# Diagonal score blocks: the lower left quarter mirrored through memory, with a new order of pairs and of the chunk steps

## The chip, the cores and the metric

One core of a Trainium2 chip runs the whole kernel. The metric is the device time of one execution in microseconds: 1388.75 us before the change, the median of three runs (1388.1 to 1389.97).

## The reference

Attention with a squared Relu, multiplied by u, then a mixture of experts in which only 80 tokens of each expert count:

```python
scores = scale * np.matmul(z, z.transpose(0, 2, 1))   # z: 8 x 2496 x 64, scale 1/2496
attn = np.maximum(scores, 0.0) ** 2
x = u * np.matmul(attn, v)                            # u, v: 8 x 2496 x 256
...
logits = x @ w_gate                                   # x as 19968 x 256, 8 experts
expert_idx = np.argmax(logits, axis=1)
gate_w = probs[np.arange(N), expert_idx]              # softmax of the logits
for e in range(E):                                    # the 80 tokens with the largest gate_w
    h = np.maximum(x[tok_idx] @ w1[e], 0.0)
    out[tok_idx] = gate_w[tok_idx, None] * (h @ w2[e])
```

The score matrix of a batch is z times its own transpose, so it is symmetric: the block of rows i and columns j is the transpose of the block of rows j and columns i.

## The kernel before

Attention fills the first 1300 us. It runs over 8 batches, in each over 5 chunks of 512 query columns (`qc`; the last one has 448), and in each chunk over 10 **steps**. A step handles one **pair** of key tiles of 128 (tiles 2p and 2p+1, step number `r`). `pairs_of` (L246) gives the order of the pairs of a chunk: 0 to 9, in the fourth chunk 8, 9, 0 to 7.

All the work of PE, ScalarE, VectorE and of SP's queue is in the order in which it is written (`manual_schedule`, L765); each engine runs its own list in order and waits by semaphores. In step i the main loop (L777) writes down first the `scores` of the pair of step i + 2 (`LOOK`), then `attend` of the pair of step i, then what is due for the chunk before (`finished`), then loads and preparations.

`scores` (L315) makes the pair's squared-Relu tile `a` (128 keys x 2 x 512 queries) and splits it in a high part `ah` and a rest `al`, so that f32 accuracy comes from reduced f32 matmuls:

- For a key tile of the chunk's own diagonal block or to the right of it: two matmuls (`zc`, `zd`: high and rest of z) into a PSUM tile `s`, Relu (ScalarE, L330), Square over both tiles (L331), `ah` as a copy (ScalarE, or VectorE where `on_v`), `al` as a subtraction (VectorE, L54).
- For a block to the left of the diagonal nothing is computed: its transpose was computed in an earlier chunk. Then `mirror` had VectorE transpose it by 32x32 (L265), `mirror_out` wrote it to memory as `y` two steps later (L275), and `mirror_back` read it again in four pieces as `blk` (L292), at most 12 steps ahead of its use, when one of four buffers is free and the write is two steps old. `mirrored` (L299) then takes only a ScalarE copy and a VectorE subtraction.

`attend` (L344) multiplies with the value tiles `vt` (also high and rest): three matmuls for each of two halves of the model dimension, 12 a step, into `acc`; the last key tile takes four instead of six. `ah` and `al` have three buffers, `a` two, `s` three.

After a chunk, `chunk_x` (VectorE, L377) multiplies `acc` with u into `xf` at step 0 of the next chunk. `finished` (L721) then spreads over the steps of the next chunk: `chunk_hi`, `chunk_rest`, `chunk_mid`, `chunk_lo` (three bf16 parts of x), `chunk_store` (two DMA transposes of `xf`, L427), `chunk_store2` (their result to memory, L436), `chunk_logits` (24 small matmuls) and `chunk_sum`. After a batch come `gate_top` (with an exponential on ScalarE, L483), `gate_near` and `gate_sum`, `count` (matmuls and a copy into `tot`), `up_to` (ten small VectorE additions) and `blocks`.

For the next batch, z is loaded (`load_z`, one buffer, L100) at step 1 and prepared at step 5 of each chunk; the value tiles are loaded (`load_v`, two buffers, L132) from the fourth chunk on and prepared (`prep_v`, a ScalarE copy and a VectorE subtraction) at steps 2, 4, 6, 8 and 9 of the fifth. `prep_u` loads u at step 2, into one buffer that `chunk_x` reads.

The last 80 us, the experts, are not touched.

## Time and profile before

| | |
|---|---|
| median of 3 runs | 1388.75 us |
| profiled execution, its own time | 1388.46 us |
| its span, first to last instruction | 1386.6 us |
| mean granted TensorE clock over the span | 0.992 |
| PE busy | 99% |
| VectorE (DVE) busy | 76% |
| ScalarE (ACT) busy | 73% |
| DMA moved | 311.89 MB |

PE is TensorE's matmuls, PEld its weight loads, DVE VectorE, ACT ScalarE, SPq the queue of SP, which issues all the large DMAs. Matmuls are pipelined and their ends are modelled, so the distance from one start to the next is what one costs. A wait is named by the instruction that waited and the one that released it.

### The profile page before, as it was taken

What the parts mean: (1) busy time and instruction counts of PE and PEld (TensorE: products, weight loads), DVE (VectorE), ACT (ScalarE), POOL (GpSimd) and SP (SyncE); (2) the same over time, 40 slices, a digit from 0 to 9 for tenths busy, and PEclk for the clock granted to TensorE, in tenths of its full rate; (3) what the DMA queues carried; (4) which work ended last, traced back from release to release, by engine and by line L of the source; (5) the groups of instructions that cost most, each with busy time, mean ns of one, the idle gap of its engine ahead of it and who ended that gap; (6) DMA issues with size and microseconds to landing.
All of it is one profiled execution on the core that took longest, in us unless ns stands there. A gap on an engine that the chain in (4) does not pass through costs nothing. (4 is left out here: it accounts for less than half of the span.)

```text
span 1386.6 us, 19562 instructions
## 1 busy us (share of the span) xinstructions
PE 1367.1 (99%) x7087; PEld 1139.5 (82%) x7087; DVE 1060.6 (76%) x1517; ACT 1008.8 (73%) x1282; POOL 36.5 (3%) x57
## 2 busy tenths in 40 slices
PE   9999999999999999999999999999999999999887
PEld 6888888888888888888888888888888888888666
DVE  8876788668877788767886688777787678867785
ACT  8866687758777587666887577775877668876375
POOL 0000000000000000000000000000000000000062
PEclk9999999999999999999999999999999999999989
DMA  6899877995888958997688958889588986789774
GB/s 223 252 249 271 225 204 239 235 267 143 256 237 231 273 151 245 239 261 197 188 252 232 270 143 259 238 225 274 145 246 239 255 210 179 220 229 252 176 225 141
DMA packets 260070, 311.89 MB, mean 225 GB/s; under 512 B 96152, under 2 KB 188192, under 8 KB 249728
## 3 DMA queue, kind: packets, MB, share of 16 engines
q1 hardware_dynamic: 258752, 309.02, 81.4%
q0 software_dynamic: 1216, 1.56, 0.4%
q8 instruction: 57, 0.93, 0.3%
q14 instruction: 45, 0.37, 0.1%
HBM read 153.48 MB, written 126.37 MB: 202 GB/s over the span
## 5 line engine op out<-in xcount | busy, mean ns | idle before, releaser
L359 PE MATMUL acc<-ah,vt 128*128 128x512 f32 (+1 forms) x1520 | 584.5, 385 | 0.3 <-DVE vt L146 0.3
L360 PE MATMUL acc<-al,vt 128*128 128x512 f32 (+1 forms) x1520 | 584.5, 385 | 0.3 <-DVE al L54 0.2
L358 PE MATMUL acc<-ah,vt 128*128 128x512 f32 (+1 forms) x1520 | 584.2, 384 | 0.0
L54 DVE TENSOR_TENSOR al<-a,ah 128x1024 fp32r<-128x1024 f32 (+1 forms) x240 | 291.5, 1214 | 135.4 <-ACT ah L105 125.6
L330 ACT ACTIVATE a<-s 128x512 f32<-128x512 f32 (+1 forms) x480 | 258.4, 590 | 153.9 <-PE s L327 143.8
L359 PEld LDWEIGHTS acc<-ah,vt 128*128 128x128 f32 x1520 | 285.4, 188 | 53.9 <-DVE vt L146 1.2
L358 PEld LDWEIGHTS acc<-ah,vt 128*128 128x128 f32 x1520 | 285.3, 188 | 52.9
L360 PEld LDWEIGHTS acc<-al,vt 128*128 128x128 f32 x1520 | 285.4, 188 | 52.9 <-DVE al L54 1.2
L331 ACT ACTIVATE a<-a 128x1024 f32<-128x1024 f32 (+1 forms) x240 | 253.0, 1054 | 7.6
L310 ACT CAST ah<-blk 128x1024 fp32r<-128x1024 f32 x160 | 167.0, 1049 | 105.6 <-PE acc L359 88.5
L54 DVE TENSOR_TENSOR al<-blk,ah 128x1024 fp32r<-128x1024 f32 x160 | 193.8, 1216 | 56.1 <-ACT ah L310 53.2
L265 DVE STREAM_TRANSPOSE x<-a 128x512 f32<-128x512 f32 x320 | 207.6, 687 | 0.0
L327 PE MATMUL s<-zd,zc 128*128 128x512 f32 (+1 forms) x480 | 186.5, 388 | 0.0
L105 ACT CAST ah<-a 128x1024 fp32r<-128x1024 f32 x153 | 160.9, 1052 | 4.8
L107 DVE CAST ah<-a 128x1024 fp32r<-128x1024 f32 (+1 forms) x87 | 59.2, 681 | 95.6 <-ACT a L331 95.6
L326 PE MATMUL s<-zc,zc 128*128 128x512 f32 x320 | 128.1, 400 | 0.0
L327 PEld LDWEIGHTS s<-zd,zc 128*128 128x128 f32 x480 | 90.3, 188 | 16.3 <-issue 0.5
L326 PEld LDWEIGHTS s<-zc,zc 128*128 128x128 f32 x320 | 60.1, 188 | 11.1
L326 PE MATMUL s<-zc 128*128 128x512 f32 (+1 forms) x160 | 63.5, 397 | 0.0
L388 ACT CAST xb<-xf 128x1024 bf16<-128x1024 f32 (+1 forms) x39 | 40.0, 1026 | 23.4 <-DVE xf L377 23.1
L396 ACT CAST xb<-xr 128x1024 bf16<-128x1024 f32 (+1 forms) x39 | 39.9, 1024 | 15.5 <-DVE xr L54 15.5
L377 DVE SCALAR_TENSOR_TENSOR xf<-acc,ut 128x512 f32<-128x512 f32 (+2 forms) x82 | 50.1, 653 | 0.0
(171 smaller groups left out, 835.9 us busy)
## 6 DMA issues: line engine op xcount, KB each, us to landing
y<-x SPq DMA_DIRECT2D x80, 1024.0 KB
blk<-y SPq DMA_DIRECT2D x320, 256.0 KB
out<-idle SPq DMA_DIRECT2D x40, 512.0 KB
vraw<-v SPq DMA_DIRECT2D x32, 512.0 KB
ut<-uT SPq DMA_DIRECT2D x32, 512.0 KB
xs<-xq SPq DMA_DIRECT2D x32, 512.0 KB
wraw<-w SPq DMA_DIRECT2D x28, 512.0 KB
zd<-zc SPq DMA_DIRECT2D x78, 128.0 KB
```

The costliest lines, as they stand in the source:

```text
L54: V.tensor_tensor(out=o, in0=a, in1=b, op=op)
L105: eng.copy(out=o, in_=i)
L107: eng.tensor_copy(out=o, in_=i)
L265: V.transpose(out=x[:, :, :, t].rearrange("p n k s -> p k n s"), in_=a)
L310: nc.scalar.copy(out=natural(ah), in_=src)
L326: nc.tensor.matmul(s[:, :nq], zk, zc[:, :nq], start=True, stop=False)
L327: nc.tensor.matmul(s[:, :nq], zk, zd[:, :nq], start=False, stop=True)
L330: nc.scalar.activation(out=a[:, h, :nq], in_=s[:, :nq], func=AF.Relu)
L331: nc.scalar.activation(out=a[:, :, :nq], in_=a[:, :, :nq], func=AF.Square)
L358: nc.tensor.matmul(o, vt[:, t, 0, cs], ah, start=k == first, stop=False)
L359: nc.tensor.matmul(o, vt[:, t, 1, cs], ah, start=False, stop=False)
L360: nc.tensor.matmul(o, vt[:, t, 0, cs], al, start=False, stop=k == last)
```

## The change

In all diagonal blocks but three (the first chunk of the first batch and the last two chunks of the last batch) the second pair's scores are computed for the right half of the block's columns only. The left half is the transpose of the right half of the first pair, which is now computed first in its chunk. VectorE transposes that half by 32x32 (`quarter_out`), SP writes it to memory at step 0 (`quarter_write`) and reads it back at step 3 (`quarter_back`), and the second pair, now the last of its chunk, takes it from there with a copy and a subtraction (`natural`).

The order of pairs in such a chunk becomes: first diagonal pair, all others, second diagonal pair. The steps of the chunk's later work move: DMA transposes from step 1 to 4, their store from 3 to 6, logits from 6 to 7 (6 after the fifth chunk), gate from 7 and 8 to 8 and 9, count from 2 to 5, prefix sums and blocks from 4 to 9. z of the next batch is loaded one chunk later (in the fifth chunk two of them); the value tiles are prepared at steps 1, 3, 6 and 8 of the fifth chunk and, the last one, at step 3 of the next batch's first chunk. `tot` is bf16, and `ex` takes the place of `lg`.

```diff
--- before.py
+++ after.py
@@ -225,7 +225,7 @@
     oh = const.tile([P, 2, NBLK, E], BF16, name="oh")
     gall = const.tile([P, NCOL - NT + 32], F32, name="gall")
     nsum = const.tile([P, B + 1], F32, name="nsum")
-    tot = const.tile([P, E, NBLK], F32, name="tot")
+    tot = const.tile([P, E, NBLK], BF16, name="tot")
     incl = const.tile([P, E, NBLK], F32, name="incl")
     rank = const.tile([P, NST, E], F32, name="rank")
     ex_last = const.tile([P, NT, E], F32, name="ex_last")
@@ -243,8 +243,19 @@
     NP = NT // 2
 
 
-    pairs_of = [list(range(NP)) for qc in range(NQ)]
-    pairs_of[NQ - 2] = [NP - 2, NP - 1, *range(NP - 2)]
+    def whole_block(b, qc):
+        return (b, qc) in ((0, 0), (B - 1, NQ - 2), (B - 1, NQ - 1))
+
+    def order(b, qc):
+        rest = [p for p in range(NP) if p // 2 != qc]
+        if whole_block(b, qc):
+            return [NP - 2, NP - 1, *range(NP - 2)] if qc == NQ - 2 else list(range(NP))
+        if qc == NQ - 2:
+            rest = rest[-2:] + rest[:-2]
+        return [2 * qc, *rest, 2 * qc + 1]
+
+    pairs_of = {(b, qc): order(b, qc) for b in range(B) for qc in range(NQ)}
+    HQ = CH // 2
     LOOK, AHEAD = 2, 12
     a_t = {}
 
@@ -254,7 +265,7 @@
     n32 = P // SQ
     now, to_write = [0], []
 
-    to_read = [(b, i, j, (b * NQ + i) * NP + pairs_of[i].index(2 * j) - LOOK)
+    to_read = [(b, i, j, (b * NQ + i) * NP + pairs_of[b, i].index(2 * j) - LOOK)
                for b in range(B) for i in range(NQ) for j in range(i)]
 
     def mirror(b, i, j, t, a):
@@ -293,6 +304,33 @@
                                   in_=y[:, :, h].rearrange("g p f -> p g f"))
             blk[b, i, j] = m
 
+    quarter = {}
+
+    def quarter_out(b, qc, a):
+
+        x = zpool.tile([P, n32, 2, 2, SQ], F32, tag="md", name=f"xd_{b}_{qc}", bufs=1)
+        for t in range(2):
+            V.transpose(out=x[:, :, :, t].rearrange("p n k s -> p k n s"), in_=a[:, t, HQ:])
+        quarter[b, qc] = now[0], x
+
+    def quarter_write():
+
+        for (b, qc), (at, x) in list(quarter.items()):
+            if at is not None and at + 2 <= now[0]:
+                y = dram.tile([n32, SQ, n32, 4 * SQ], F32, tag="yd", name=f"yd_{b}_{qc}", bufs=2)
+                nc.sync.dma_start(out=y.rearrange("g p h f -> (g p) (h f)"),
+                                  in_=x.rearrange("p h k t s -> p (h k t s)"))
+                quarter[b, qc] = None, y
+
+    def quarter_back(b, qc):
+
+        _, y = quarter.pop((b, qc))
+        m = zpool.tile([P, n32, 2, 2 * SQ], F32, tag="md", name=f"md_{b}_{qc}", bufs=1)
+        for h in range(n32):
+            nc.sync.dma_start(out=m[h * SQ:(h + 1) * SQ].rearrange("p g k f -> p g (k f)"),
+                              in_=y[:, :, h].rearrange("g p f -> p g f"))
+        quarter[b, qc] = None, m
+
     def pair_tile(tag, b, qc, k, dt=F32R, bufs=3):
         return ew.tile([P, 2, CH], dt, tag=tag, name=f"{tag}_{b}_{qc}_{k}", bufs=bufs)
 
@@ -318,22 +356,35 @@
             return mirrored(b, qc, k)
         nq = min(CH, seq - qc * CH)
         zc, zd = zc_t[b, qc], zd_t[b, qc]
+        diag = k // QT == qc and not whole_block(b, qc)
+        lower = diag and k % QT > 0
+        c0, c1 = (HQ, nq) if lower else (0, CH if diag else nq)
         a = pair_tile("a", b, qc, k, F32, 2)
         ss = []
         for h in range(2):
             zk = zc_t[b, k // QT][:, (k % QT + h) * P:(k % QT + h + 1) * P]
             s = ps_s.tile([P, CH], F32, tag="s", name=f"s_{b}_{qc}_{k + h}")
-            nc.tensor.matmul(s[:, :nq], zk, zc[:, :nq], start=True, stop=False)
-            nc.tensor.matmul(s[:, :nq], zk, zd[:, :nq], start=False, stop=True)
+            nc.tensor.matmul(s[:, c0:c1], zk, zc[:, c0:c1], start=True, stop=False)
+            nc.tensor.matmul(s[:, c0:c1], zk, zd[:, c0:c1], start=False, stop=True)
             ss.append(s)
         for h, s in enumerate(ss):
-            nc.scalar.activation(out=a[:, h, :nq], in_=s[:, :nq], func=AF.Relu)
-        nc.scalar.activation(out=a[:, :, :nq], in_=a[:, :, :nq], func=AF.Square)
+            nc.scalar.activation(out=a[:, h, c0:c1], in_=s[:, c0:c1], func=AF.Relu)
+        nc.scalar.activation(out=a[:, :, c0:c1], in_=a[:, :, c0:c1], func=AF.Square)
         ah = pair_tile("ah", b, qc, k)
+        al = pair_tile("al", b, qc, k)
+        if lower:
+            m = quarter.pop((b, qc))[1].rearrange("p n k (t s) -> p k t n s", t=2)
+
+            def natural(o):
+                return o[:, :, :HQ].rearrange("p k (t n s) -> p k t n s", t=2, s=SQ)
+
+            nc.scalar.copy(out=natural(ah), in_=m)
+            tt(natural(al), m, natural(ah), ALU.subtract)
         on_v = k // QT == qc or (qc, k) in ON_V and b > 0
-        cp(V if on_v else nc.scalar, ah[:, :, :nq], a[:, :, :nq])
-        al = pair_tile("al", b, qc, k)
-        tt(al[:, :, :nq], a[:, :, :nq], ah[:, :, :nq], ALU.subtract)
+        cp(V if on_v else nc.scalar, ah[:, :, c0:nq], a[:, :, c0:nq])
+        tt(al[:, :, c0:nq], a[:, :, c0:nq], ah[:, :, c0:nq], ALU.subtract)
+        if diag and not lower:
+            quarter_out(b, qc, a)
         if k // QT > qc:
             for h in range(2):
                 mirror(b, k // QT, qc, k % QT + h, a[:, h])
@@ -343,7 +394,7 @@
 
     def attend(b, qc, k, cols=range(DC)):
         nq = min(CH, seq - qc * CH)
-        first, last = 2 * pairs_of[qc][0], 2 * pairs_of[qc][-1] + 1
+        first, last = 2 * pairs_of[b, qc][0], 2 * pairs_of[b, qc][-1] + 1
         if k == first:
             acc_t[b, qc] = [ps_a.tile([P, CH], F32, tag="acc", name=f"acc_{b}_{qc}_{c}")
                             for c in range(DC)]
@@ -479,7 +530,7 @@
         last = b == B - 1
         d = d_last if q1 == NQ and last else small("d")
         tt(d, lg, bc(mx), ALU.subtract)
-        ex = ex_last[:, q0 * QT:q1 * QT] if last else small("ex")
+        ex = ex_last[:, q0 * QT:q1 * QT] if last else lg
         nc.scalar.activation(out=ex, in_=d, func=AF.Exp)
 
         fw = small("fw")
@@ -685,6 +736,9 @@
     RAW = {(qz, 4): (2, 1), None: (2, 2)}
     WARM = 3, 6
     WARM0 = 8
+    keys_in = {qc: [(qc - 1, 1, 6)] for qc in range(1, NQ)}
+    keys_in[0] = []
+    keys_in[NQ - 1] = [(NQ - 2, 1, 4), (NQ - 1, 4, 7)]
     steps = [(b, qc, r) for b in range(B) for qc in range(NQ) for r in range(NP)]
     ET = mybir.EngineType
     v_raw, z_raw, w_raw = {}, {}, {}
@@ -725,28 +779,28 @@
             chunk_hi(b, qc)
         elif r == 2:
             chunk_rest(b, qc)
-        if r == (3 if at_end else 1):
+        if r == (3 if at_end else 4):
             chunk_store(b, qc)
-        if r == (5 if at_end else 3):
+        if r == (5 if at_end else 6):
             chunk_store2(b, qc)
         if r == (2 if at_end else 3):
             chunk_mid(b, qc)
         if r == (3 if at_end else 4):
             chunk_lo(b, qc)
-        if r == (5 if at_end else 6):
+        if r == (5 if at_end else 6 if qc == NQ - 1 else 7):
             chunk_logits(b, qc)
             chunk_sum(b, qc)
         kb = b * BPB
         if b < B - 1 and qc == NQ - 1:
-            if r == 7:
+            if r == 8:
                 gate_top(b, 0, NQ)
-            elif r == 8:
+            elif r == 9:
                 gate_sum(b, gate_near(b, 0), gp)
         elif qc == 0 and b > 0:
             part = kb - BPB, kb
-            if r == 2:
+            if r == 5:
                 count(*part)
-            elif r == 4:
+            elif r == 9:
                 up_to(*part)
                 blocks(ps_m, "m", gp, oh, *part)
         elif at_end:
@@ -781,7 +835,7 @@
                 prep_zc(0, r // 2 + 2, z_raw.pop((0, r // 2 + 2)))
             if i + LOOK < len(steps):
                 nb, nqc, nr = steps[i + LOOK]
-                scores(nb, nqc, 2 * pairs_of[nqc][nr])
+                scores(nb, nqc, 2 * pairs_of[nb, nqc][nr])
             if r == 0 and prev:
                 chunk_x(*prev)
             if b == 0 and qc == 0:
@@ -792,7 +846,7 @@
                         v_raw[0, g + 1] = load_v(0, g + 1)
                 if r == 8:
                     constants_v()
-            p = pairs_of[qc][r]
+            p = pairs_of[b, qc][r]
             for k in (2 * p, 2 * p + 1):
                 if not last or k < NT - 3:
                     attend(b, qc, k)
@@ -803,19 +857,22 @@
             if r == 2:
                 prep_u(b, qc)
             if b + 1 < B:
-                if r == 1:
-                    z_raw[b + 1, qc] = load_z(b + 1, qc)
-                if r == 5:
-                    prep_zc(b + 1, qc, z_raw.pop((b + 1, qc)))
+                for j, load, prep in keys_in[qc]:
+                    if r == prep:
+                        prep_zc(b + 1, j, z_raw.pop((b + 1, j)))
+                    if r == load:
+                        z_raw[b + 1, j] = load_z(b + 1, j)
                 if qc == NQ - 2 and r in (2, 4):
                     g = r // 2 - 1
                     v_raw[b + 1, g] = load_v(b + 1, g)
                 if qc == NQ - 1:
-                    g = (r - 1) // 2 if r < 9 else 4
-                    if r in (2, 4, 6, 8, 9):
+                    if r in (1, 3, 6, 8):
+                        g = (1, 3, 6, 8).index(r)
                         prep_v(b + 1, g, v_raw.pop((b + 1, g)), nc.scalar, V)
                         if g + 2 < NQ:
                             v_raw[b + 1, g + 2] = load_v(b + 1, g + 2)
+            if b and qc == 0 and r == 3:
+                prep_v(b, NQ - 1, v_raw.pop((b, NQ - 1)), nc.scalar, V)
             if nb < B and r == 1:
                 prep_zd(nb, nqc)
             if r == 5 and b < B - 1:
@@ -826,6 +883,9 @@
                 weights_ahead(qc, r)
             mirror_back()
             mirror_out()
+            quarter_write()
+            if r == 3 and not whole_block(b, qc):
+                quarter_back(b, qc)
             if r == NP - 1:
                 prev = b, qc
 
```

## Rows read from the trace of the kernel before

**Rows 1.** The page: busy time (share) x instructions of each engine; DMA packets.

```profile
PE 1367.1 (99%) x7087; PEld 1139.5 (82%) x7087; DVE 1060.6 (76%) x1517; ACT 1008.8 (73%) x1282; POOL 36.5 (3%) x57
...
DMA packets 260070, 311.89 MB, mean 225 GB/s; under 512 B 96152, under 2 KB 188192, under 8 KB 249728
```

**Rows 2.** Windows, fourth batch: stretch, busy us (x instructions), clock, DMA share, GB/s.

```profile
495.90:530.60 34.70, 34.70 (x176) 28.66 (x174) 29.14 (x43) 28.63 (x38) 0.00 (x0) 1.00 0.65 180
...
599.60:628.90 29.30, 29.30 (x152) 24.19 (x151) 20.27 (x22) 15.29 (x18) 0.00 (x0) 1.00 0.98 274
628.90:657.90 29.00, 29.00 (x164) 26.44 (x163) 22.63 (x25) 21.30 (x27) 0.00 (x0) 1.00 0.72 193
10.00:1290.00 1280.00, 1279.58 (x6553) 1072.56 (x6552) 983.74 (x1308) 948.86 (x1181) 0.00 (x0) 1.00 0.84 228
```

**Rows 3.** Timeline of PE, 512 columns: start, length; first and last of ten.

```profile
599.83 0.39 PE L359 MATMUL acc<-ah,vt 128*128 128x512 f32 x1
...
601.87 0.39 PE L359 MATMUL acc<-ah,vt 128*128 128x512 f32 x1
```

**Rows 4.** Windows, third chunk of the fourth batch: tile acc, then tile s.

```profile
564.90:599.60 34.70, 28.02 (x119) 22.14 (x118) 1.28 (x2) 1.00 0.93 236
...
564.90:599.60 34.70, 8.65 (x32) 5.93 (x32) 0.00 (x0) 8.69 (x16) 1.00 0.93 236
```

**Rows 5.** Timeline of PE, experts, 256 columns: first and last of nine.

```profile
1347.62 0.28 PE L1196 MATMUL op<-w2l,hTh 128*80 128x256 f32 x1
...
1348.57 0.28 PE L1196 MATMUL op<-w2h,hTh 128*80 128x256 f32 x1
```

**Rows 6.** Timeline of PE, 448 columns: first and last of eleven.

```profile
639.83 0.36 PE L358 MATMUL acc<-ah,vt 128*128 128x448 f32 x1
...
641.85 0.36 PE L359 MATMUL acc<-ah,vt 128*128 128x448 f32 x1
```

**Rows 7.** Timeline of PE, 8 columns; then the page: weight loads of scores.

```profile
1306.24 0.83 PE L416 MATMUL pl<-wg_sb,xf 128*128 128x8 f32 x6 [1.20 <-DVE xf L377]
...
L327 PEld LDWEIGHTS s<-zd,zc 128*128 128x128 f32 x480 | 90.3, 188 | 16.3 <-issue 0.5
```

**Rows 8.** Groups by form: busy us, mean ns of one, idle before.

```profile
L330 ACT ACTIVATE a<-s 128x512 f32<-128x512 f32 x448 | 242.8, 594 | 132.3 <-PE s L327 122.2 <-DVE x L265 8.2
L331 ACT ACTIVATE a<-a 128x1024 f32<-128x1024 f32 x224 | 237.8, 1061 | 7.1
...
L265 DVE STREAM_TRANSPOSE x<-a 128x512 f32<-128x512 f32 x320 | 207.6, 687 | 0.0
L107 DVE CAST ah<-a 128x1024 fp32r<-128x1024 f32 x71 | 49.2, 693 | 84.1 <-ACT a L331 84.1
L54 DVE TENSOR_TENSOR incl<-incl,tot 128x8 f32<-128x8 f32 x77 | 13.5, 175 | 2.4
```

**Rows 9.** Tile blk: who waited for its reads (us, times).

```profile
  ACT ah L310: 5.0, 7
```

**Rows 10.** Waits of SP's queue: us in total, times, longest.

```profile
SPq L427 <- DVE xf L377: 202.9, 25, 14.0
SPq L292 <- DMA y<-x: 179.5, 38, 8.7
```

**Rows 11.** Timeline of ACT at the gate of the third batch.

```profile
528.06 0.34 ACT L483 ACTIVATE ex<-d 128x160 f32<-128x160 f32 x1 [3.07 <-DVE d L54]
528.30 1.99 ACT L310 CAST ah<-blk 128x1024 fp32r<-128x1024 f32 x2
```

**Rows 12.** Timeline of ACT: the last value tile's copies.

```profile
494.77 1.43 ACT L105 CAST vt<-vraw 128x768 fp32r<-128x768 f32 x3
```

**Rows 13.** Timeline of SP's queue, third chunk of the fourth batch.

```profile
565.75 1.83 SPq L292 DMA_DIRECT2D blk<-y  x4
568.09 9.13 SPq L427 DMA_TRANSPOSE xq<-xf  x2
```

**Rows 14.** Timeline of SP's queue, fourth chunk.

```profile
620.39 0.44 SPq L132 DMA_DIRECT2D vraw<-v  x1
```

## Prediction

> **What bounds the kernel now.** I read the page's busy shares first: TensorE is busy 99% of the span, at a granted clock of 1.00 (the 2.4 GHz level) up to 1290 us, VectorE and ScalarE stand near 75% [rows 1, 2]. A busy share of PE proves little, since a 512-column matmul is drawn 0.39 us long though the next one starts after 0.227 us [rows 3]. So I counted. The stretch of the third chunk of the fourth batch lasts 34.70 us and holds 118 value matmuls and 32 score matmuls [rows 4]; 150 x 0.2267 = 34.0 us, and the 24 small logits matmuls fill the rest. There is no idle time to recover: from 10 to 1290 us the kernel lasts exactly as long as its matmul starts. VectorE and ScalarE are under 85% in the stretches shown [rows 2], so what counts is (a) how many matmul columns go away, and (b) whether ScalarE, VectorE, the DMA engines and SP's queue still deliver each pair in time. Their work is worth nothing by itself.
>
> **What is removed: score columns.** 37 of the 40 diagonal blocks are changed (all but (0,0), (7,3), (7,4)). In each, the second pair's four score matmuls (two key tiles, hi and lo) run over the right half only.
> - Chunks 0 to 3: 30 blocks x 4 = 120 matmuls go from 512 to 256 columns. 512 columns cost (601.87 - 599.83) / 9 = 0.2267 us [rows 3]. The nearest row for 256 columns of the same type is the experts' second product: (1348.57 - 1347.62) / 8 = 0.119 us [rows 5]. 120 x 0.108 = 12.9 us.
> - Chunk 4: 7 x 4 = 28 matmuls go from 448 to 192 columns. 448 cost (641.85 - 639.83) / 10 = 0.202 us [rows 6]. By columns 192 would cost under 0.1, but six 8-column matmuls with a full 128x128 f32 weight load take 0.83 us, of which some 0.26 is the last one's own length: 0.57 / 5 = 0.114 us each [rows 7]. I take that as the floor of a load: 28 x 0.088 = 2.5 us.
> - Chunk 4's first pair now writes all 512 columns instead of 448: 28 x 0.025 = 0.7 us back.
>
> Sum: 12.9 + 2.5 - 0.7 = **14.7 us off TensorE**. The 256-column row has weights of 80 columns, ours have 128; the floor of 0.114 lies under 0.119, so I keep 0.119. From both sides: half of 0.2267, 0.113, would give 13.6 + 2.5 - 0.7 = 15.4 in all. The load itself is drawn 0.188 us long [rows 7], and if none of that could be hidden behind so short a matmul, 120 x 0.039 + 28 x 0.014 - 0.7 = 4.4 would be left. 0.119 is the nearest row by far.
>
> The Trainium skill speaks against these prices ("TensorE: Matmul & The Clock Gate", section "Back-to-back issue gap"): it gives a sustained stream 131 ns for 512 columns and 81 ns for 128. By it, halving would save some 33 ns, an estimate between its two figures, and 148 matmuls some 5 us, near the far end of rival 3 below. The row shows 227 ns for this stream of f32 matmuls with a weight load each, so measurement and page differ, and the rows decide.
>
> **What is added, and what hides it.** None of it is on TensorE.
> - ScalarE, per block: two Relus and one Square over half (0.594 x 2 and 1.061 [rows 8] lose about half, 1.0 us), one copy of the mirrored quarter added (512 of 1024 elements, 0.6 us). Net a small gain.
> - VectorE, per block: two half transposes added (0.69 each for 512 columns [rows 8], so 0.7 us together), the cast halves (-0.3), the subtraction is cut in two (+0.1). Net +0.5 us, 18 us over the kernel, on an engine with 5.6 to 9.0 us idle in the stretches shown [rows 2].
> - DMA, per block: 256 KB out, 256 KB back, 0.52 MB; 37 x 0.52 = 19.4 MB on 311.9 [rows 1], 6%. The fourth chunk already runs at 0.98 and 274 GB/s; 0.52 MB at that rate is 1.9 us more than it has room for. The fifth runs at 0.72 [rows 2], with 8 us free, and takes the overflow. Who suffers are the block reads; ScalarE waited before 7 of their 160 copies, 5.0 us in all [rows 9]. With the diagonal pair first, nearly all these reads are used one step later than now: 2.4 us more cover.
> - SP: one more write, at step 0 of the chunk, and four reads at step 3; use is at step 7. From write to use lie seven steps of at least 12 x 0.202 = 2.4 us, 17 us. SP is in order and waits at step 3 for the write to land; the longest such wait for a mirrored block is 8.7 us [rows 10], counted from two steps after its write. Here three steps have passed, so little is left. From the reads to the use: four steps, 10 to 11 us.
>
> **What is moved.**
> - Order of pairs: diagonal pair first, its partner last. At each chunk's end the light lower pair (ScalarE about 1.8 us instead of 2.2) precedes the next chunk's diagonal pair and two mirrored ones (except in chunk 0); the burst of eight off-diagonal pairs in chunk 0 stays. There a pair costs ScalarE 2 x 0.59 + 1.06 + 1.05 = 3.3 us (Relus, Square, cast; the cast as long as the copies of [rows 11]) against a PE step of 16 x 0.2267 = 3.63. Eight pairs leave 2.6 us, plus 1.05 for the one cast that is on VectorE, less 2.0 for the two bf16 casts of the chunk before: 1.6 us. Moving the last value tile's preparation into this burst takes 1.43 us [rows 12] of it. Over the whole stretch there is more room: 28.63 of 34.70 us busy [rows 2]. If the cover is gone, a local excess of under 1 us a batch is the price.
> - The gate's exponential makes ScalarE wait 3.07 us for VectorE [rows 11]. At step 8 it stands between the next chunk's diagonal pair and its first mirrored pair. From that step's start: scores 0.9, Relus and Square 2.2, cast, subtraction, transposes and two small operations 3.3 (6.4), exponential and copy 1.3 (7.7) [rows 11], subtraction 1.2 (8.9). Needed after 3.18 + 2.72 + 2.72 + 0.91 + 0.45 = 10.0 us. One microsecond to spare.
> - Ten prefix sums of 0.175 us [rows 8] move to step 9, ahead of a chunk_x: 1.75 us where I count 2 to spare. The bf16 totals change these by less than their own length, on VectorE.
> - DMA transposes from step 1 to step 4, store from 3 to 6. In the third chunk they held SP for 9.13 us behind two block reads [rows 13]; now the u load, the next z and zd and the quarter's read are ahead of them. Behind them are a z load (chunk 4: needed three steps later, 7 us or more) and v loads (six steps). xf must be read before the next chunk_x, six steps or 15 us on; 9.1 us fits.
>
> What would be late next is therefore ScalarE in chunk 0 and SP's queue in the fourth chunk, both still inside their cover.
>
> **The sum.** The profiled execution took 1388.46 us (span 1386.6), 0.29 under the median of 1388.75. 1388.75 - 14.7 = **1374.1 us**.
>
> **Rivals.**
> 1. Small new waits, each chunk or batch: the three points with about 1 us to spare turn out a little short. 0.5 to 1 us at one point a batch to two a batch is 3.5 to 14 us; around 7: 1381. For it: the short margins above. Against: no PE wait of this kind in 1280 us of before.
> 2. Slower: SP falls behind in the fourth chunk. Before, the v load of step 4 left at 620.39 [rows 14], when PE (chunk begun at 599.6, steps of 2.3 to 2.7 us) was in step 7: three steps late. If SP is as late at the quarter's read in step 3, the read leaves in step 6; four issues take 1.8 us (as four reads in [rows 13]) and after landing the pair needs about 2.8 us on ScalarE and VectorE, before the start of step 9. A landing of 4 to 8 us then makes PE wait 1 to 5 us in each of seven fourth chunks, and the fifth chunks, with shorter steps and their own lag, as much: 14 places x 2.5 = 35 us, **1409**. It turns slower than before from 1.1 us a place. Against: half of that lag came from the two transposes at step 1 and their wait for xf (SP waited 202.9 us for it in all [rows 10]), and these now come behind the read.
>    The Trainium skill has a rule on this side ("DMA: Bandwidth & Descriptors", section "Rules for kernel authors"): transfers should be coalesced, and under 64 KB one pays mostly overhead. The quarter comes back in four pieces of just 64 KB; no row shows their landing.
> 3. A half-width matmul isn't half the price, because a 128-column load can't hide behind it as the 80-column one of the row does: midway between 0.119 and 0.188, 0.153 us, 120 x 0.073 + 28 x 0.049 - 0.7 = 9.4 come off, 1379.3; at 0.188, 4.4 and 1384.3. Against: 0.114 in [rows 7].
>
> **How the numbers follow.** Forecast with no new wait worth a microsecond a batch, 1372.0 to 1376.5: 0.60. Rival 1, up to 1384: 0.20, and up to 1388: 0.03. Rival 3: 0.05, of which 0.01 for its far end. Rival 2: 0.09. Better than 1372.0 (0.113 a matmul, and small late starts gone): 0.03. The range takes in the forecast, rival 3 and the likelier half of rival 1: 1372.0 to 1381.5. About 0.2% (2.8 us) is what a measurement of this kernel can tell from no change. Faster by more: 0.60 + 0.20 + 0.05 + 0.03 = 0.88. Within: 0.04. Slower: 0.08.
>
> **What would show it.** In the trace after: score matmuls 256 columns wide, 120 of them, some 0.119 us from start to start (step of the price right); stretches of about 0.43 us less per chunk; still no idle time ahead of value matmuls. Wrong it is if PE shows waits at the last pair of a chunk for the cast or subtraction of the mirrored quarter (rival 2), or at the second pair of a batch's second chunk (the exponential), or if SP's waits on the quarter's write reach many microseconds.

## The result, and the profile after

The changed kernel takes 1374.59 us (median of 5 runs, 1373.87 to 1375.52) against 1388.75 us (median of 5 runs, 1387.84 to 1390.15): 14.2 us less, a ratio of 0.9899 with a 95% interval of 0.9889 to 0.991. The forecast was 1374.1. The profiled execution took 1374.59 us (span 1372.9).

The page of the changed kernel, busy time of each engine and the DMA packets:

```profile
PE 1353.9 (99%) x7086; PEld 1128.6 (82%) x7087; DVE 1078.0 (79%) x1628; ACT 992.5 (72%) x1319; POOL 37.8 (3%) x57
...
DMA packets 286715, 331.33 MB, mean 241 GB/s; under 512 B 99113, under 2 KB 210097, under 8 KB 276369
```

Against [rows 1], TensorE still fills 99% of the span and has as many matmuls, but 13.2 us less busy time. ScalarE lost 16 us, VectorE gained 17, and the DMA engines move 19.4 MB more.

Windows of the fourth batch after the change: its first, fourth and fifth chunk, and the whole batch (stretch, its length, busy us of PE, PEld, DVE, ACT and POOL with instructions, granted clock, DMA share as the profile gives it, also above 1, GB/s):

```profile
490.20:524.50 34.30, 34.30 (x176) 28.42 (x175) 29.43 (x42) 27.84 (x40) 0.00 (x0) 1.00 0.86 257
593.60:622.40 28.80, 28.80 (x151) 23.85 (x150) 21.11 (x27) 16.01 (x21) 0.00 (x0) 1.00 1.06 276
622.40:650.30 27.90, 27.90 (x160) 25.41 (x159) 22.90 (x28) 20.05 (x25) 0.00 (x0) 1.00 1.04 268
490.20:650.30 160.10, 160.10 (x837) 134.63 (x836) 127.61 (x183) 117.30 (x156) 0.00 (x0) 1.00 0.92 247
```

The same whole batch in the kernel before:

```profile
495.90:657.90 162.00, 162.00 (x837) 136.03 (x836) 124.58 (x168) 119.36 (x150) 0.00 (x0) 1.00 0.83 227
```

The batch has the same 837 matmuls and is 1.90 us shorter. PE is busy in all of it, at full granted clock, in both kernels. DMA changed more than the time did: the fourth chunk, full before [rows 2], stays at 276 GB/s, and the fifth goes from 193 to 268 GB/s.

Timeline of PE after, the four score matmuls of a lower pair (the second diagonal pair), first with 256 columns (third chunk), then with 192 (fifth chunk), each time the first of the four and the value matmul behind them; start, length as drawn, operation:

```profile
581.90 0.28 PE L367 MATMUL s<-zc 128*128 128x256 f32 x1
...
582.38 0.40 PE L409 MATMUL acc<-ah,vt 128*128 128x512 f32 x1
...
639.45 0.25 PE L367 MATMUL s<-zc 128*128 128x192 f32 x1
...
639.87 0.39 PE L409 MATMUL acc<-ah,vt 128*128 128x448 f32 x1
```

256 columns go at (582.38 - 581.90) / 4 = 0.120 us, 192 columns at (639.87 - 639.45) / 4 = 0.105 us, against 0.2267 and 0.202 for the full widths [rows 3, 6]. Over all 120 matmuls of 256 columns the mean is 0.123 us, because seven of them take 0.20; over the 28 of 192 columns it is 0.106.

The waits for the mirrored quarter after the change (engine, line, what it waited for: us in total, times, longest):

```profile
DVE al L54 <- ACT ah L381: 36.5, 12, 6.4
ACT ah L381 <- DMA md<-yd: 28.3, 12, 4.6
...
PE acc L409 <- DVE ah L107: 0.4, 1, 0.4
...
SPq L330 <- DMA yd<-xd: 5.3, 2, 3.4
```

ScalarE (L381 copies the quarter) finds it not yet landed in 12 of 37 blocks, all of them in fourth and fifth chunks. Almost none of that comes through: PE waits once for a lower pair, 0.43 us, in the batch where ScalarE waited longest. SP (L330 reads the quarter back) waits for the write of the quarter to land at 2 of the 37 reads.

### The profile page after: what moved, and what is told of

Same layout as the page of the kernel before. It is cut to its first block, busy times and chain, and to the rows that moved or that the text cites. A ratio compares the mean times of both kernels' runs of the same rounds, so it can differ in the third digit from the quotient of the medians.

```text
span 1372.9 us, 19936 instructions
## 1 busy us (share of the span) xinstructions
PE 1353.9 (99%) x7086; PEld 1128.6 (82%) x7087; DVE 1078.0 (79%) x1628; ACT 992.5 (72%) x1319; POOL 37.8 (3%) x57
## 5 line engine op out<-in xcount | busy, mean ns | idle before, releaser
L54 DVE TENSOR_TENSOR al<-a,ah 128x1024 fp32r<-128x1024 f32 (+1 forms) x240 | 271.8, 1132 | 140.2 <-ACT ah L105 135.4
L371 ACT ACTIVATE a<-s 128x512 f32<-128x512 f32 x480 | 243.3, 559 | 118.1 <-PE s L368 113.0
L372 ACT ACTIVATE a<-a 128x1024 f32<-128x1024 f32 x240 | 237.9, 991 | 7.6
L368 PE MATMUL s<-zd,zc 128*128 128x512 f32 x480 | 177.3, 373 | 0.2 <-DVE zd L54 0.2
L107 DVE CAST ah<-a 128x1024 fp32r<-128x1024 f32 (+3 forms) x87 | 49.0, 563 | 28.2 <-ACT a L372 27.8
L54 DVE TENSOR_TENSOR al<-md,ah 128x512 fp32r<-128x512 f32 x37 | 25.4, 686 | 41.1 <-ACT ah L381 36.5
L146 DVE TENSOR_TENSOR vt<-vraw,vt 128x1024 fp32r<-128x1024 f32 (+1 forms) x40 | 46.1, 1152 | 12.5 <-ACT vt L105 12.4
```

Source lines behind the costliest of these rows:

```text
L54: V.tensor_tensor(out=o, in0=a, in1=b, op=op)
L107: eng.tensor_copy(out=o, in_=i)
L368: nc.tensor.matmul(s[:, c0:c1], zk, zd[:, c0:c1], start=False, stop=True)
L371: nc.scalar.activation(out=a[:, h, c0:c1], in_=s[:, c0:c1], func=AF.Relu)
L372: nc.scalar.activation(out=a[:, :, c0:c1], in_=a[:, :, c0:c1], func=AF.Square)
```

## The experiments

The theory from the trace: all of the gain is the score columns taken away; the moved steps gain nothing and only keep the added work hidden. Each kernel was timed beside the kernel before on the same chip, so ratios are compared. The changed kernel itself, run again:

> The changed kernel once more, as the measure for the three kernels beside it: 1374.6, within 0.7.

1374.58 us, ratio 0.9901 (0.9881 to 0.9922).

### Are the columns the whole gain?

**Order and steps alone**, every diagonal block computed whole:

```diff
-        diag = k // QT == qc and not whole_block(b, qc)
+        diag = False
...
-            quarter_write()
-            if r == 3 and not whole_block(b, qc):
-                quarter_back(b, qc)
```

> The new order of pairs and all moved steps, but every diagonal block is computed whole: no quarter, no trip through memory. Theory (only matmul columns count): 1388.7 us, within 1.0. Rival (the order and the moved steps carry part of the gain, or cost something): more than 1.5 us away from 1388.7, either way. DMA falls back to about 312 MB.

1388.10 us, ratio 0.9996 (0.9987 to 1.0006). The moved steps by themselves are worth nothing either way.

**Everything of the change but the narrow matmuls.** The lower pair's matmuls run over all columns again, their left half is not used:

```diff
+            m0 = 0 if lower else c0
-            nc.tensor.matmul(s[:, c0:c1], zk, zc[:, c0:c1], start=True, stop=False)
-            nc.tensor.matmul(s[:, c0:c1], zk, zd[:, c0:c1], start=False, stop=True)
+            nc.tensor.matmul(s[:, m0:c1], zk, zc[:, m0:c1], start=True, stop=False)
+            nc.tensor.matmul(s[:, m0:c1], zk, zd[:, m0:c1], start=False, stop=True)
```

> The changed kernel, but the second pair's score matmuls run over all columns of the block; the left half of the result is not used, the quarter still comes through memory. Theory (only matmul columns count): 1374.6 + 14.7 - 0.7 for chunk 4's wider first pair left in = 1389, within 1.5, with no gain left from ScalarE's halved work. Rival (halved Relus, Squares and casts carry part of the gain): 1385 or less.

1387.98 us, ratio 0.9994 (0.9984 to 1.0004). The page of this kernel, busy times:

```profile
PE 1368.4 (99%) x7086; PEld 1140.3 (82%) x7087; DVE 1079.1 (78%) x1628; ACT 995.3 (72%) x1319; POOL 38.0 (3%) x57
```

VectorE, ScalarE and the trip through memory are as in the changed kernel; PE's busy time is up by 14.5 us and the whole gain is gone. (The 14.7 of the expectation already has the 0.7 taken off. By its terms 12.9 + 2.5 come back, 1390.0, and 2 us less was measured.)

**The narrow matmuls alone**, put into the kernel before with its order and steps; the left half of the lower pair is filled from the right half or with zeros, so the mirrored values are left out:

```diff
+            lower = k // QT == qc and k % QT > 0 and (b, qc) not in (
+                (0, 0), (B - 1, NQ - 2), (B - 1, NQ - 1))
+            c0 = CH // 2 if lower else 0
-            nc.tensor.matmul(s[:, :nq], zk, zc[:, :nq], start=True, stop=False)
-            nc.tensor.matmul(s[:, :nq], zk, zd[:, :nq], start=False, stop=True)
+            nc.tensor.matmul(s[:, c0:nq], zk, zc[:, c0:nq], start=True, stop=False)
+            nc.tensor.matmul(s[:, c0:nq], zk, zd[:, c0:nq], start=False, stop=True)
...
```

> The kernel before with its own order and steps, only the second pair's score matmuls made as narrow as in the change (30 blocks 256, 7 blocks 192 columns); the left half of the pair's tile is filled from the right half (in chunk 4 with zeros), so a quarter of these blocks is wrong, and nothing goes through memory for it. Theory (only matmul columns count): 1388.75 - 12.9 - 2.5 = 1373.3, within 1.0. Rival (the new order is needed to keep the pairs in time): 1377 or more.

1374.17 us, ratio 0.9893 (0.9875 to 0.9911): the gain of the whole change, with neither its new order nor its trip. Three kernels pin the time to the columns within about 1 us.

### What does the trip through memory cost?

**No trip:** the quarter is taken straight from the transposed tile, without write and read, so the reordering that the trip does is left out:

```diff
-            m = quarter.pop((b, qc))[1].rearrange("p n k (t s) -> p k t n s", t=2)
+            m = quarter.pop((b, qc))[1].rearrange("p n k t s -> p k t n s")
...
-            quarter_write()
-            if r == 3 and not whole_block(b, qc):
-                quarter_back(b, qc)
```

> The changed kernel without the trip: ScalarE and VectorE take the second pair's left half from the 32x32-transposed tile itself, so its values stand in the wrong places, and the write to memory and the read back are left out. Theory (the trip is covered): only the two PE waits of 0.25 and 0.43 us seen in the changed kernel's trace go, 0 to 1 us less than the changed kernel. Rival (the trip's 19 MB cost time): 3 us or more less.

1373.51 us, ratio 0.989 (0.987 to 0.9909), 1.1 us under the changed kernel run beside it, and the two ranges of times overlap. The 37 writes and 148 reads of 64 KB are covered to within about 1 us.

**The read one step earlier** (step 2 instead of 3):

```diff
-            if r == 3 and not whole_block(b, qc):
+            if r == 2 and not whole_block(b, qc):
```

> The changed kernel, the quarter read back at step 2 instead of 3. Theory: ScalarE's 28.3 us of waiting for the quarter shrink to under 10 us, and the time stays within 1 us, since these waits reached PE only once. Rival (SP then stands at the write's landing and delays what is behind it): as many ScalarE waits, for the quarter or for mirrored blocks, and 1 us or more longer.

1374.58 us, ratio 0.9889 (0.9869 to 0.9909), the time of the changed kernel. Four waits of this kernel, and its read of the quarter in the fourth chunk of the fourth batch, which starts at 593.8 (start, time the queue was held, operation):

```profile
ACT ah L381 <- DMA md<-yd: 18.3, 9, 5.3
...
DVE zc L112 <- DMA zraw<-zT: 12.6, 7, 3.7
...
PE acc L409 <- DVE ah L107: 1.2, 1, 1.2
...
SPq L330 <- DMA yd<-xd: 16.0, 9, 4.5
```

```profile
606.00 3.93 SPq L330 DMA_DIRECT2D md<-yd  x4
```

The expected drop to under 10 us did not come. ScalarE waits 10 us less for the quarter, and all of that lies in fifth chunks (1.1 us instead of 10.7); in fourth chunks it is 17.2 instead of 17.5 us. There the read leaves 12.2 us after the start of the chunk in both kernels (the changed one's row stands below, at 605.80): in SP's order the u load, which waits for `chunk_x`, a value load, a block read and a y write stand ahead of it at step 2 as at step 3. Only in the seventh batch it leaves earlier, by 0.3 us. So this run does not show what an earlier read is worth where cover is thin. Of what the rival expected, SP now stands 16.0 us at the quarter's write instead of 5.3, and the next z tile lands later (12.6 us of waits against 7.0), but the time does not grow. One wait reaches PE, 1.2 us, behind ScalarE's longest, 5.3.

**The read two steps later** (step 5):

```diff
-            if r == 3 and not whole_block(b, qc):
+            if r == 5 and not whole_block(b, qc):
```

> The changed kernel, the quarter read back at step 5 instead of 3. Theory (cover is counted in steps): in chunks 0 to 2 the read still ends some 8 us before its use and nothing changes; in the fourth it comes about 5.4 us later where PE has 2 to 4 us left, in the fifth 4.9 us later: PE waits 2 to 4 us in 15 places, 30 to 60 us, about 1415. Rival (the DMA engines' backlog, not SP's place in the order, sets the landing): under 1380.

1458.56 us, ratio 1.0507 (1.0489 to 1.0525). Waits of PE, then of ScalarE, in this kernel:

```profile
PE acc L409 <- DVE ah L107: 60.2, 7, 9.7
PE s L367 <- ACT a L371: 3.5, 4, 0.9
...
ACT ah L381 <- DMA md<-yd: 116.8, 14, 13.8
```

SP's queue in the fourth chunk of the fourth batch, which starts at 627.3 here:

```profile
639.50 9.11 SPq L478 DMA_TRANSPOSE xq<-xf  x2
...
652.63 3.32 SPq L330 DMA_DIRECT2D md<-yd  x4
```

The place is as expected, the size is not: seven waits of 7.4 to 9.7 us, each at the last pair of a fourth chunk. The read at step 5 stands behind the two transposes of step 4, a value load and a block read; it leaves 25.3 us after the start of the chunk (23.3 to 25.4 in the seven fourth chunks), 11 to 13 us later than in the changed kernel, where 5.4 was expected. In the first three chunks of a batch the quarter is in time. ScalarE's waits in fifth chunks reach PE only through the four short ones, each in the first chunk of the next batch. The waits make 64 us of the 82 us that the span grew; most of the rest is the clock, below.

### Why the DMA transposes stand at the fifth pair

**Transposes back at step 1, store at step 3:**

```diff
-        if r == (3 if at_end else 4):
+        if r == (3 if at_end else 1):
             chunk_store(b, qc)
-        if r == (5 if at_end else 6):
+        if r == (5 if at_end else 3):
             chunk_store2(b, qc)
```

> The changed kernel with the DMA transposes back at step 1 and their store at step 3. Theory (SP's queue is the thin cover): the transposes stand ahead of the quarter's read at step 3, so in the fourth and fifth chunks, where ScalarE already waits 0.9 to 4.6 us for the quarter, it comes 2 to 6 us later and PE waits 0 to 4 us in each: 1374.6 + 5 to 30 us, about 1385. Rival (the move of the transposes is not needed): 1374.6 within 1.0.

1412.35 us, ratio 1.0165 (1.0148 to 1.0182): slower than before, and by far more than the 10 us I expected. SP's queue in the fourth chunk of the fourth batch (start, time the queue was held, operation), first in the changed kernel, whose chunk starts at 593.60:

```profile
600.23 0.39 SPq L159 DMA_DIRECT2D ut<-uT  x1
...
603.52 1.76 SPq L303 DMA_DIRECT2D blk<-y  x4
605.33 0.43 SPq L286 DMA_DIRECT2D y<-x  x1
605.80 3.47 SPq L330 DMA_DIRECT2D md<-yd  x4
610.02 4.99 SPq L478 DMA_TRANSPOSE xq<-xf  x2
```

and with the transposes at step 1, where the chunk starts at 610.00:

```profile
616.10 2.69 SPq L478 DMA_TRANSPOSE xq<-xf  x2
...
624.75 0.75 SPq L487 DMA_DIRECT2D xs<-xq  x1
625.54 7.82 SPq L330 DMA_DIRECT2D md<-yd  x4
```

The four reads of the quarter are issued from 12.2 to 15.7 us after the start of the chunk in the one, from 15.5 to 23.4 us in the other. The first of them leaves 3.3 us later, and the issue itself stretches from 3.47 to 7.82 us. From there to the matmul, ACT, DVE and then PE of the kernel with transposes at step 1:

```profile
637.82 0.62 ACT L381 CAST ah<-md 128x512 fp32r<-128x512 f32 x1 [7.46 <-DMA md<-yd]
...
638.47 0.69 DVE L54 TENSOR_TENSOR al<-md,ah 128x512 fp32r<-128x512 f32 x1 [9.24 <-ACT ah L381]
639.08 0.42 DVE L107 CAST ah<-a 128x512 fp32r<-128x512 f32 x1
...
639.64 0.76 PE L409 MATMUL acc<-ah,vt 128*128 128x512 f32 x1 [3.32 <-DVE ah L107]
640.21 0.63 PE L410 MATMUL acc<-ah,vt 128*128 128x512 f32 x1
640.63 0.63 PE L411 MATMUL acc<-al,vt 128*128 128x512 f32 x1
```

VectorE runs its list in order: the subtraction of the mirrored quarter waits 9.24 us for ScalarE's late copy, and the cast of the right half (L107) stands behind it. So PE's wait is named for that cast and not for the quarter, two engines back. After the wait the matmuls start 0.42 us apart instead of 0.2267. Windows of this kernel around it (columns as in the windows above; the granted clock stands behind the five engines):

```profile
610.00:639.10 29.10, 26.33 (x139) 21.46 (x137) 16.49 (x20) 13.54 (x18) 0.00 (x0) 0.99 1.00 272
639.10:646.00 6.90, 6.36 (x16) 5.10 (x17) 4.97 (x10) 3.36 (x4) 0.00 (x0) 0.53 1.07 269
646.00:650.00 4.00, 4.00 (x21) 3.71 (x21) 3.44 (x4) 2.35 (x3) 0.00 (x0) 1.00 1.00 210
```

The second window begins 0.5 us before the end of the wait; its granted clock of 0.53 is about the lower of the two levels (1.2 GHz). The 16 matmuls that start in it, twelve with 512 and four with 448 columns, take 6.39 us from 639.64 to the next start at 646.03; at 0.2267 and 0.202 they would take 3.53, so 2.9 us are lost on top of the wait. The same sum at the seven places of PE's timeline gives 1.5 to 3.0 us, 15 in all. The seven waits make 23.6 us of idle time (2.8 to 4.4 each), or 24.7 as the starts were delayed: 40 together, against 41.1 by which this kernel's span is longer than the changed one's. With the read at step 5 the seven places lose 1.4 to 2.5 us behind their waits, 13 in all, of the 18 us that the waits leave over.

**The same, with the quarter's read at step 2.** Transposes and store as in the last diff, and

```diff
-            if r == 3 and not whole_block(b, qc):
+            if r == 2 and not whole_block(b, qc):
```

> The transposes at step 1 as in e4_transposes_1, but the quarter read back at step 2 instead of 3, ahead of a block read, a y write and the store that then stood before it in SP's queue. Theory (the place in SP's queue decides): the read leaves 3 to 6 us earlier in the fourth chunk, PE waits there fall to under 1 us each, 1375 to 1380. Rival (the transposes' own load on the DMA engines decides): most of the waits stay, 1395 or more.

1389.13 us, ratio 1.0003 (0.9992 to 1.0014), between what the theory and its rival expected. Waits of PE, this kernel:

```profile
PE acc L409 <- DVE ah L107: 10.0, 7, 2.1
```

The reads leave about 15 us after the start of the chunk, hardly earlier than with the read at step 3: in SP's order only the store moves behind them, the block read and the y write stay ahead. Their issue is over at 19 to 20 us instead of 22 to 23. So putting the read ahead of the store takes back 23 of the 38 us. The seven waits are 0.6 to 2.1 us long. Behind five of them 0.3 us is lost, behind two (2.1 and 1.8 us long) 1.9 each, at the lower clock; another wait of 1.8 us is among the five. What is left can come from the place behind the transposes in SP's order or from what transposes and store put on the DMA engines while the quarter is read; the two were not separated.

**Transposes late in the fourth chunk alone**, at step 1 in all others:

```diff
-        if r == (3 if at_end else 4):
+        early = qc != NQ - 3
+        if r == (3 if at_end else 1 if early else 4):
             chunk_store(b, qc)
-        if r == (5 if at_end else 6):
+        if r == (5 if at_end else 3 if early else 6):
             chunk_store2(b, qc)
```

> DMA transposes at step 1 and their store at step 3 as in e4_transposes_1, except while the fourth chunk runs, where they stay at steps 4 and 6. Theory (only the fourth chunk lacks cover): the seven PE waits of 3 to 4.6 us of e4_transposes_1 go and 1374.6 within 1.5 is left. Rival (the transposes' place matters in every chunk, by the DMA backlog they leave): 1380 or more.

1382.81 us, ratio 0.9951 (0.9932 to 0.9969): 8 us lost where none was expected. The waits of fourth chunks are gone, but others come. PE's waits for ScalarE in attention, this kernel:

```profile
PE s L367 <- ACT a L371: 3.8, 5, 0.9
```

The timeline of its ScalarE and PE at the start of a batch:

```profile
187.53 1.44 ACT L105 CAST vt<-vraw 128x768 fp32r<-128x768 f32 x3
188.88 1.07 ACT L371 ACTIVATE a<-s 128x512 f32<-128x512 f32 x2
...
189.51 0.50 PE L367 MATMUL s<-zc,zc 128*128 128x512 f32 x1 [0.91 <-ACT a L371]
```

With the transposes at step 1 of the fifth chunk the quarter comes late there: ScalarE waits up to 4.7 us for it (3.5 in the changed kernel), and PE's five waits, 0.4 to 0.9 us, follow the four fifth chunks in which it waited 4.0 us or more. In the rows above ScalarE is about 2 us behind in the next batch's first chunk (the value tile's copies start at 187.53, in the changed kernel at 185.18), and in the burst of computed pairs, which holds the last value tile's copies, it has not made that up. Matmul starts in attention account for some 5.7 of the 8 us; the other 2.4 lie in the experts' part and were not explained.

### Why the logits and the gate are later

**All four steps back**: logits to 6, gate to 7 and 8, counts to 2, prefix sums to 4:

```diff
-        if r == (5 if at_end else 6 if qc == NQ - 1 else 7):
+        if r == (5 if at_end else 6):
...
-            if r == 8:
+            if r == 7:
                 gate_top(b, 0, NQ)
-            elif r == 9:
+            elif r == 8:
...
-            if r == 5:
+            if r == 2:
                 count(*part)
-            elif r == 9:
+            elif r == 4:
```

> The changed kernel with logits at step 6, the gate at steps 7 and 8, the count at 2 and the prefix sums at 4, as before. Theory (these steps are covered wherever they stand): 1374.6, within 1.0. Rival (they were moved because PE would wait for them): 1377 or more, with PE waits in each batch's first or second chunk.

1382.23 us, ratio 0.9947 (0.993 to 0.9963). The theory said 1374.6 and fell; the rival, at least 1377, held. **The same with the gate alone at its new steps 8 and 9**, the other three at the old ones:

```diff
-        if r == (5 if at_end else 6 if qc == NQ - 1 else 7):
+        if r == (5 if at_end else 6):
...
-            if r == 5:
+            if r == 2:
                 count(*part)
-            elif r == 9:
+            elif r == 4:
```

> e5_old_logits with the gate alone back at the change's steps 8 and 9 (logits at 6, count at 2, prefix sums at 4 as before the change). Theory (the gate's exponential at step 7 stood between ScalarE and the next chunk's first pair, which is a computed one now): the waits of 0.77 and 0.28 us per batch go, 1374.6 within 1.0. Rival (the count or the prefix sums cost it): 1380 or more.

1375.63 us, ratio 0.9894 (0.9877 to 0.991). That is 0.03 us outside the expected 1.0. So the gate's step was worth 7 us, and the other three nothing that can be told from no change. ScalarE at the gate, first with the gate at step 7, then in the changed kernel:

```profile
200.82 0.34 ACT L534 ACTIVATE lg<-d 128x160 f32<-128x160 f32 x1 [3.17 <-DVE d L54]
201.07 1.06 ACT L371 ACTIVATE a<-s 128x512 f32<-128x512 f32 x2
```

```profile
199.01 1.09 ACT L371 ACTIVATE a<-s 128x512 f32<-128x512 f32 x2 [1.19 <-PE s L368]
200.13 1.06 ACT L372 ACTIVATE a<-a 128x1024 f32<-128x1024 f32 x1
204.53 0.34 ACT L534 ACTIVATE lg<-d 128x160 f32<-128x160 f32 x1 [3.33 <-DVE d L54]
204.77 1.98 ACT L348 CAST ah<-blk 128x1024 fp32r<-128x1024 f32 x2
```

The exponential waits as long in both, 3.2 and 3.3 us. At step 7 the next chunk's diagonal pair queues behind it: with the new order of pairs this is a computed pair, which needs Relus and Square at once. At step 8 it has already passed, and a mirrored pair follows, which has the slack. What arrives late with the gate at step 7, on VectorE and then on PE:

```profile
204.06 1.23 DVE L54 TENSOR_TENSOR al<-a,ah 128x1024 fp32r<-128x1024 f32 x1
...
204.34 0.40 PE L410 MATMUL acc<-ah,vt 128*128 128x512 f32 x1
205.34 0.50 PE L411 MATMUL acc<-al,vt 128*128 128x512 f32 x1 [0.60 <-DVE al L54]
...
208.91 0.39 PE L410 MATMUL acc<-ah,vt 128*128 128x512 f32 x1
209.38 0.50 PE L411 MATMUL acc<-al,vt 128*128 128x512 f32 x1
```

The subtraction ends just as the matmul at 205.34 starts, 1.00 us after the one before it instead of 0.23; from 204.08 to 206.85 eight starts take 2.77 us where 1.81 is their pitch. That is 0.96 us. A second late start follows in the next step (209.38, 0.47 us after the one before it); there 0.35 us more are lost. 1.31 us in each of seven batches is 9.2, against 9.0 by which the span of this profiled execution is longer than the changed kernel's; the medians differ by 7.6.

## Why the prediction was right, step by step

- **The bound** (PE lasts as long as its matmul starts, other engines are worth nothing by themselves): shown by the three kernels on columns, order and trip. ScalarE's 16 us of saved work and VectorE's 17 us of added work are both without effect.
- **The price.** 0.119 for 256 columns measured 0.120. The floor of 0.114 for 192 columns was too high, 0.105 measured: I took it from 8-column matmuls whose last one's length I had to guess [rows 7]. With the measured pitches 120 x 0.1067 + 28 x 0.097 - 0.7 = 14.8 us against 14.7; a full batch 4 x 0.43 + 0.29 = 2.0 against 1.90 in the windows. With the means over all of them it is 14.4. 14.2 was measured, less than 1 us off and inside the spread.
- **Rival 3** (half the width is not half the price) is refuted by the same rows. The Trainium skill's figures for a sustained stream, which I weighed there, do not hold for this one. Its formula for a single matmul in the same section of "TensorE: Matmul & The Clock Gate", "Back-to-back issue gap" (columns at 2.4 GHz and 2.5 ns), gives by my estimate 216, 109 and 82 ns for 512, 256 and 192 columns: near 227 and 120 measured, and too low for the narrowest, at 105.
- **Trip and SP's order.** Right that the trip is covered and that SP hardly waits for the quarter's write to land: 2 of the waits at L330 in the changed kernel name it, 5.3 us, the others are for other transfers in the main. Wrong in how much cover is left. "From the reads to the use: four steps, 10 to 11 us" counted from the step at which the read stands in the program; it leaves SP 12.2 us after the start of the chunk, about a step late, and is issued in 3.47 us, where I took 1.8. The delay arises ahead of the read: the u load waits for `chunk_x` and leaves 6.6 us after the start of the chunk, and four block reads follow; the prediction names the u load there but counts no wait for it. ScalarE waited 28.3 us for the quarter, against 5.0 for all block reads before [rows 9], and one of these waits came through to PE, by 0.43 us. That no more came through is in part luck: the margin that held was not the one worked out.
- **DMA load.** Right that the full fourth chunk passes its overflow on to the fifth, but "with 8 us free" was too much: its share went from 0.72 to 1.04. How much of that is overflow, and how much the fifth chunk's own quarter and the z load that moved there, was not separated.
- **Rival 2** did not come about, for the reason given: the transposes stand behind the read. With the transposes at step 1 the time is 1412.35, close to the 1409 of that rival, by another sum: seven places and not fourteen, 3.4 us of wait each and not 2.5, and a loss by the clock that I had not counted at all. The Trainium skill's rule that transfers under 64 KB are mostly overhead ("DMA: Bandwidth & Descriptors", "Rules for kernel authors") ends at just the size of these pieces. No run here shows their overhead, only that writes and reads together cost about 1 us of the kernel's time.
- **Rival 1**, the three points of about 1 us to spare. The gate's exponential: the point was rightly found, and no wait of PE stands there at step 8, while one step earlier costs 7 us. ScalarE's burst in the first chunk: 0.2 us to spare by my count, and no PE wait there in the fourth batch; one of 0.25 us in the seventh, after the longest wait in a fifth chunk (3.46 us), and five of 0.4 to 0.9 us when the transposes make more fifth chunks late. So this margin is as thin as it was worked out. The prefix sums cost nothing, at step 9 or at step 4.

## What to carry to other kernels

When an engine is busy to the last instruction, count its work in start-to-start times: taking columns away paid its counted price. Of the rest of the change, the places of the transposes, of the quarter's read and of the gate keep that from being lost; the moved logits, counts and prefix sums show no effect, and the moved z and value tiles were not tested alone. A read with a deadline belongs ahead of bulk work in an in-order queue, and its cover is to be counted from when the queue lets it go under load, not from where it stands in the program. A wait on ScalarE that cannot be avoided goes where a pair with slack comes next.

## What the runs showed of the hardware that I had not expected

- A wait on TensorE can cost more than its length. Behind a wait of 3.32 us the matmuls ran at the lower clock (0.53 granted over 6.9 us), which added 2.9 us; behind waits of 7.4 to 9.7 us it was no more, 1.4 to 2.5 us. Of two waits of 1.8 us one was followed by the lower clock and 1.9 us of loss, the other by the full clock and 0.3. After the 0.6 us waits at the gate the pitch was back at 0.23 within three matmuls. The Trainium skill ("TensorE: Matmul & The Clock Gate", "What's actually happening") has two levels, of which the lower one comes after idle time, and the trace agrees for the long waits.
- The time for which issues hold SP's queue is not told by their number, nor by the DMA share of the chunk: four reads of 64 KB took 3.47 us in the changed kernel and 7.82 us with the transposes at step 1, in fourth chunks with shares of 1.06 and 1.00.
- Two transposes held SP's queue for 9.13 us before [rows 13], 4.99 us in the changed kernel, 2.69 us when issued at step 1 of a fourth chunk and 9.11 us with the read at step 5: it is no fixed price, and what sets it was not separated.
